# Block transposes of k and x in one VectorE step, exchanged through DRAM, with a new order of work, in an RWKV recurrence fused with a token and channel mixer

## The chip, the cores and the metric

The kernel runs on one core of a Trainium2 chip. The metric is device microseconds of that core, the median of the runs. A core has TensorE (PE in the profile; its weight loads are PEld), VectorE (DVE), ScalarE (ACT), GpSimd (POOL) and SyncE (SP), which here only issues DMAs. Each works through its own list of instructions in order, and waits for the others by semaphores.

## The reference

Four batches, eight heads, 768 steps, 48 channels a head; all is f32.

```python
for t in range(S):
    cur = np.einsum('bhd,bhe->bhde', u[None] * kt, vt)
    y[:, :, t] = np.einsum('bhd,bhde->bhe', rt, state + cur)
    state = wt[:, :, :, None] * state + np.einsum('bhd,bhe->bhde', kt, vt)
...
xt = x.transpose(0, 2, 1)                 # x = y as (4, 768, 384)
h = xt @ U @ V                            # token mix, rank 32
u = x + h.transpose(0, 2, 1)
ch = np.maximum(u @ w_ch1, 0.0) @ w_ch2   # channel mix, 384 -> 1536 -> 384
return (u + ch)
```

## The kernel before

The recurrence is done in 24 chunks of 128 steps (batch b, chunk c, number g = 6b + c), each for all heads: the eight heads lie in pairs j = 0..3, two heads on 128 partitions. For a chunk VectorE makes products of the decays by scans (steps F and Q, lines 390 and 405), r and k are scaled by them (RP, KS), TensorE makes the scores (AM, line 544), VectorE merges them under a mask (CP, line 551), and TensorE makes y from them and v (YA, lines 622 and 632) and from the state of the chunks before (YZ, lines 645 and 649). ScalarE copies y out as x with channels on partitions (XE). The new state needs k with time on partitions: DS (line 561) multiplies it by v, one matmul for each head, with 48 columns of k as the stationary operand; then ZA and ZM add the old state and decay it. The last chunk of a batch makes no state.

Two things are therefore turned from channels-by-time to time-by-channels: k of each chunk for DS (20 chunks), and x of each chunk for the token mix (GA, line 761, then G4, SELM, GS, GSL, once a batch). There are two ways. For early chunks TensorE turns them by transposing matmuls (KT line 522, XT line 735) and ScalarE copies the result out (KN, XN). For the chunks in `TURN_K_DVE` and `TURN_X_DVE`, here 12 to 23, VectorE turns them by blocks of 32 x 32: `turn_blocks` (line 679) and `blocks_of_x` (lines 714 and 716) do a 128 x 128 tile in four steps of four instructions, each from 32 partitions to 32 others, so that each block is turned and put in its place at once.

The 3072 rows of x are cut into seven blocks of 384 or 512 for the channel mix. For each block HP (line 815) makes the token mix, VectorE adds it to x (UADD, line 820), u is split into a high and a low part (UH, UL), UP (line 864) makes 12 products of 9 matmuls, each followed by a ReLU split into high and low (HH on ScalarE line 869 or VectorE line 871, HL line 875), and DN (line 898) makes 3 x 4 products of 9 matmuls, then O (line 916) adds u and OUT sends it. Weights are loaded and split into two parts on the way (LRAW, E, C2, C3, ADD, HI, SUB), and looked at once more later (LCK, CK, CM).

The program is written as some 1400 named steps, each with its engine and the buffers that it takes. The table `ORDER` gives the order in which they are issued, and for each whether it goes to its first engine or to the other one. `plan` replays it: it hands out buffers and refuses an order in which something stands ahead of what it needs. So the order on each engine, SP's DMAs among them, is fixed by hand.

Of the kernel before, what the change touches and what calls it, by code (L numbers as in the profile page):

```python
# [8 lines left out]
F32 = mybir.dt.float32  # L9
# [33 lines left out]
TURN_K_DVE, TURN_X_DVE = [12, 13, 14, 15, 16, 17, 18, 19, 20, 21, 22, 23], [12, 13, 14, 15, 16, 17, 18, 19, 20, 21, 22, 23]  # L43
# [5 lines left out]
def channel_order():  # L49
# [17 lines left out]
    "4S00907X04500D04o15704415804605305400G07Z00A01C00B17v05004q059G0m00X05500H04c04T01A18204704r00e00n00I17u04V0"  # L67
# [3 lines left out]
    "5b11P00k01317w07r08L01f08418A07s08V11K01e01W07t08W11L05l08907p11g00x05m05+08101M08P09e01h05-05o01X08X01N05n0"  # L71
    "8506005p11i05q08615f00y01r01O15c01Y01R01Z08711S01Q08B06102A05g08w01a09E01T08Q05h08S08C01b05d08n08F08T01j08G0"
    "6205e01U01k02B08m08Y16S06309n05x06T08x15r02305y08Z11c15i08o02C01l01s01V15s01t08R02D01u02E05z05u01m05j01y05t0"
    "1n08O01o08p05v05k08c01v05w08u16408a01w06701p08r01x08b01q02402O08D08d01+08y12506501-08E18H06A01z06802H06B0660"
    "2006W09M08v02F02I02608s08z06X08t02706C02102212j02J08+12808e02G18h02P02K08q18i02V02L09206909h08f09009C06a06U0"
# [12 lines left out]
    "G90Az0A+0Do0GA0Dm0Dn0GC0A-0G31GS0G-0I10Dp0Dq0GG0Dr0Ds0Av0B10Dt0Ku0Du0Gv0Gw1Dy0B20Dv0Dw0Dz0D+0GD0E00B30Dx0GB0"
    "E10D-0Gt0Lj0LW0Li0GE0GH0Gc0E20H30LX0B40E30GT1EG0Ga0GV0Gx0LS0E40H41GO0IS0Gu0EH1HM0B50EJ0EI0Gy0GF0E50E60EK0EM0"
    "IT0II0IU0Kw0EL0Ew0Gd0EN0B00Gb1HP0Ge0Lq0G+0EO0EV0Kv0GI0Gf0LT0HQ0Gz1GK0LJ0Ex0H60Gg0EW0Eb0HN0Ec0Aw0ES0EX0Ed0HZ0"  # L90
    "B60IL0E70GJ1EA0E80GL0H50Gh0Gl0LK0Gm0I20Lr0Gi0IV0HA0HU0H70E90H80HR0EB1EP0EC0HS0ED0LL0LU0Ey0ET0Hu0HO0EU0Ls0EQ0"
    "EE1ER0HT0HV0Ha1EY0Gj0L70Hs0Ee0EF0EZ0Ef0HB0Ea0Hc0Gk1Gn0Hb1E+0E-0I30Hv0F00Eg0Hd0Eh0HF0Hx0HG0H90IJ0HC0Hg0HH0Ez1"
    "Ht0L90Ei0Go0He0Ek0Hf0Hh0El0Em0H+1HI0HJ0HD0HK0Hy0Ln0En0F20Eq0F30L80F40I60F10Er0Lt0IK0Gp0Gq0Eo0IW0Hz1I70F50Es0"
    "Hw1FI0Et0I80Hi0I41HL0IA0IX1Eu0Hl0FJ1L40HE1I51Hm0FL0FK0IN0I90IO0F90Ep0FM1Ev0IQ0IP1FR0Hj0IB0IY0Lo0Hk0IC0Gr0FA0"
    "Ej0FN0Hn0FS1IF0FB0ID0Ho0IG0F60IM1Hp0F70F80IZ0FX0FT0FF0Hq0LA0K+0IE1IH0FY0FZ0FO0FG1FH0Hr0Ia0Ib0FP0L50Ih0FC0Ic0"
    "FQ0Id0FD0Lv0Ie0FE0If0Fa0Ig0Fg0Ii0L60Ij0Fb0Ik0Il0LC0Lu0LY0Fc0Im0Fh0In0Ir0Io0Jp0Ip0La0Is0Jq0Iv0Iw0Jt0FU0Ju0FV0"
    "It1FW0Fd0Fe1Iq1M00Fi0Iu0Ff0Fj0Fm0Fn0Fo0Fp0Fq0M20LZ0Fs0Ft0Kx0IR0Ix1Fk0M10Kz0LM0LD0Ky0Iy1Fu0Fv0JC0Kr0Jr0JD1JE0"
    "JR0JS1Lw0Fw0J00Iz0JT0Lz0J11Lp0Kt0J20I+0Jx0JF0I-0JG1J90JH0Jy0LF0JL0JA1J30JB0LN0Lx0LB0Ks0Jv1JM0JU0J40J50L10Js1"
    "JO0JV1Ly0JN0JW0JI0JJ1J60JK0K-0LP0JX0JP1J70J80LE0JQ0Jw0Jz1JY0H-0JZ0Ja0J+1Jd0Je0Jf0Jg0Jj0Jh0Jb0LQ0KQ0Jk0KK0KR1"
# [1125 lines left out]
```

## Time and profile before

| what | us |
|---|---|
| median of 3 runs | 434.61 |
| lowest and highest of them | 434.53, 435.64 |
| span of the profiled execution, first to last instruction | 433.5 |
| PE busy, share | 418.0, 96% |
| PEld busy, share | 363.0, 84% |
| DVE busy, share | 351.0, 81% |
| ACT busy, share | 185.5, 43% |
| POOL busy, share | 134.3, 31% |

The profile gives no separate time of its own execution beside the span; the median of the runs is 1.1 us above it. Its part 2 shows DVE at 9 tenths or more in nearly every slice up to 320 us and at 2 to 7 tenths after that, PE at 9 tenths from 55 us to the end. The granted TensorE clock is 1.00 from 60 us on and 0.94 ahead of that. A busy PE is not a PE at its peak, so what PE could do is read from the starts of its matmuls.

### The profile page before, as it was taken

What the parts mean: (1) busy time and instruction counts of PE and PEld (TensorE: products, weight loads), DVE (VectorE), ACT (ScalarE), POOL (GpSimd) and SP (SyncE); (2) the same over time, 40 slices, a digit from 0 to 9 for tenths busy, and PEclk for the clock granted to TensorE, in tenths of its full rate; (3) what the DMA queues carried; (4) which work ended last, traced back from release to release, by engine and by line L of the source; (5) the groups of instructions that cost most, each with busy time, mean ns of one, the idle gap of its engine ahead of it and who ended that gap; (6) DMA issues with size and microseconds to landing.
All of it is one profiled execution on the core that took longest, in us unless ns stands there. A gap on an engine that the chain in (4) does not pass through costs nothing. (4 is left out here: it accounts for less than half of the span.)

```text
span 433.5 us, 10486 instructions
## 1 busy us (share of the span) xinstructions
PE 418.0 (96%) x4156; PEld 363.0 (84%) x4156; DVE 351.0 (81%) x802; ACT 185.5 (43%) x527; POOL 134.3 (31%) x178
## 2 busy tenths in 40 slices
PE   7987999999999999999999999999989999999994
PEld 5976789999998998787778788888767899999994
DVE  8999999998999999999999999999974237325510
ACT  5999889766443343643044254040332012103400
POOL 5665455635735494322238101041000000000000
PEclk9989899999999999999999999999999999999999
DMA  8989638355826464003226403233002041136001
GB/s 279 327 267 338 204 132 310 110 198 172 272 80 217 123 242 158 23 26 107 98 64 231 119 23 117 81 119 122 8 30 74 1 162 39 36 104 206 2 2 60
DMA packets 23913, 57.29 MB, mean 132 GB/s; under 512 B 2864, under 2 KB 7856, under 8 KB 23856
## 3 DMA queue, kind: packets, MB, share of 16 engines
q1 hardware_dynamic: 23856, 56.54, 39.3%
q8 instruction: 34, 0.56, 0.5%
q14 instruction: 23, 0.19, 0.1%
HBM read 51.81 MB, written 4.72 MB: 130 GB/s over the span
## 5 line engine op out<-in xcount | busy, mean ns | idle before, releaser
L898 PE MATMUL f<-hid,w2h 128*128 128x384 f32 (+1 forms) x504 | 148.5, 364 | 0.0
L864 PE MATMUL f<-u,w1h 128*128 128x384 f32 (+1 forms) x504 | 147.8, 364 | 0.6 <-DVE xT L820 0.3
L864 PEld LDWEIGHTS f<-u,w1h 128*128 128x128 f32 x504 | 92.9, 188 | 12.9 <-issue 1.4
L898 PEld LDWEIGHTS f<-hid,w2h 128*128 128x128 f32 x504 | 92.9, 188 | 10.2 <-issue 0.7
L864 PE MATMUL f<-u,w1l 128*128 128x384 f32 (+1 forms) x252 | 90.8, 360 | 0.0
L898 PE MATMUL f<-hid,w2l 128*128 128x384 f32 (+1 forms) x252 | 90.7, 360 | 0.0
L869 ACT ACTIVATE hid<-f 128x384 fp32r<-128x384 f32 (+1 forms) x60 | 32.2, 538 | 96.9 <-PE f L864 88.9
L875 DVE SCALAR_TENSOR_TENSOR hid<-f,hid 128x384 fp32r<-128x384 f32 (+1 forms) x84 | 50.0, 608 | 11.2 <-ACT hid L869 10.5
L898 PEld LDWEIGHTS f<-hid,w2l 128*128 128x128 f32 x252 | 47.4, 188 | 4.7
L864 PEld LDWEIGHTS f<-u,w1l 128*128 128x128 f32 x252 | 47.4, 188 | 4.0
L679 DVE STREAM_TRANSPOSE kn<-rk 32x128 f32<-32x128 f32 x160 | 48.3, 302 | 2.5
L469 ACT ACTIVATE A<-ident,dv 128x128 f32<-128x128 f32 x140 | 43.8, 391 | 6.0 <-DVE dv L455 4.0
L916 DVE TENSOR_TENSOR xT<-f,xT 128x384 f32<-128x384 f32 (+1 forms) x21 | 12.7, 610 | 38.0 <-PE f L898 37.9
L831 POOL TENSOR_TENSOR u<-xT,u 128x512 fp32r<-128x512 f32 (+1 forms) x10 | 12.3, 1238 | 91.5 <-PE f L864 35.8
L322 POOL TENSOR_TENSOR cva_w<-cva_w,raw_w 128x384 int32<-128x384 int32 x24 | 25.0, 1055 | 41.1 <-DVE cva_w L315 15.7
L405 DVE TENSOR_TENSOR_SCAN Q<-w,starts,qd 128x258 f32<-128x258 f32 x48 | 33.3, 735 | 0.5 <-POOL rk L413 0.2
L551 DVE COPY_PREDICATED A<-maskf,aps 128x1024 f32<-128x1024 uint32 x24 | 31.6, 1315 | 0.4 <-PE aps L544 0.2
L390 DVE TENSOR_TENSOR_SCAN F<-w,qd 128x259 f32<-128x259 f32 x48 | 30.4, 675 | 0.5 <-DMA w<-in_wT 0.4
L716 DVE STREAM_TRANSPOSE xn<-xT 32x192 f32<-32x192 f32 x80 | 29.5, 369 | 1.1
L413 POOL TENSOR_TENSOR rk<-rk,Q 128x512 f32<-128x512 f32 x18 | 21.5, 1193 | 25.4 <-DVE Q L405 25.4
L871 DVE TENSOR_SCALAR hid<-f 128x384 fp32r<-128x384 f32 (+1 forms) x24 | 14.3, 596 | 17.7 <-PE f L864 14.4
L475 POOL TENSOR_SCALAR_AFFINE_SELECT A<-dv 128x128 f32<-128x128 f32 (+1 forms) x39 | 11.7, 333 | 43.1 <-DVE dv L455 20.0
(126 smaller groups left out, 568.2 us busy)
## 6 DMA issues: line engine op xcount, KB each, us to landing
raw_w<-in_w SPq DMA_DIRECT2D x48, 384.0 KB, 3.8
rk<-in_rkT SPq DMA_DIRECT2D x24, 512.0 KB, 5.4
kr<-in_rkN SPq DMA_DIRECT2D x18, 384.0 KB, 4.1
w<-in_wT SPq DMA_DIRECT2D x24, 260.0 KB, 4.0
v<-in_vS SPq DMA_DIRECT2D x24, 224.0 KB, 4.6
out_dram<-xT SPq DMA_DIRECT2D x12, 192.0 KB, 3.5
out_dram<-xT SPq DMA_DIRECT2D x9, 256.0 KB, 4.7
raw_V<-in_V SPq DMA_DIRECT2D x8, 96.0 KB, 3.8
```

The lines of the kernel that those rows point to most:

```text
L322: lambda: nc.gpsimd.tensor_tensor(out=d["to"].bitcast(I32), in0=d["a"].bitcast(I32), in1=d["e"], op=ALU.add),
L390: nc.vector.tensor_tensor_scan(out=back(F), data0=back(st["w"]), data1=back(qd, OVER * h), initial=1.0, op0=ALU.mult, op1=ALU.add)
L405: nc.vector.tensor_tensor_scan(out=st["Q"][:, a:e], data0=st["w"][:, a:e], data1=qd[:, a - OVER * h : e - OVER * h], initial=starts[:, h : ...
L413: ENG[eng].tensor_tensor(out=rk[:, 0], in0=rk[:, 0], in1=Qv, op=ALU.mult)
L469: nc.scalar.activation(to, one, AF.Copy, scale=dv[:, NP * i + j : NP * i + j + 1])
L551: nc.vector.copy_predicated(to, mask2, new)
L679: nc.vector.transpose(to[32 * j : 32 * j + 32, :, 32 * i : 32 * i + 32], src[32 * i : 32 * i + 32, :, 32 * j : 32 * j + 32])
L716: nc.vector.transpose(to[q, :, :, r], src[r, :, :, q])
L864: nc.tensor.matmul(ps, wt[:, f, ct, :], u[ct][:, z], start=(m == 0), stop=(m == 8))
L869: nc.scalar.activation(h[:, 0], d["ps", f], AF.Relu)
L875: nc.vector.scalar_tensor_tensor(out=h[:, 1], in0=d["ps", f], scalar=0.0, in1=h[:, 0].bitcast(F32), op0=ALU.max, op1=ALU.subtract)
L898: nc.tensor.matmul(d["o", ct], wt[:, 4 * ct + part, f - 3 * part, :], hid[f][:, z], start=(part == 0 and m == 0), stop=(part == 3 and m == 8),
```

## The change

k of chunks 9, 10, 12 to 16 and 18 to 22, and x of chunks 9 to 23, are now turned in three steps. One VectorE instruction turns each 32 x 32 block where it lies, on all 128 partitions (KB for k; XB1 or XB2 for x of one or two chunks). One DMA writes that to a tile in DRAM (KW, XW), and four DMAs read it back with the blocks exchanged (KL, XL). The turned tiles are laid out by quarters of the channels, so DS takes 32 channels at a time: 16 matmuls with 32 stationary columns in place of 8 with 48. GA reads x in the new layout and GS puts its columns back in order. Chunks 9 to 11 thereby leave TensorE's transposes. On PE the table differs from the fourth UP product of block 0 on. `CHOICES` lets a step have more than one other engine, which no step here uses, and the step that loads the flag (PF) must now stand ahead of the last O.

```diff
-TURN_K_DVE, TURN_X_DVE = [12, 13, 14, 15, 16, 17, 18, 19, 20, 21, 22, 23], [12, 13, 14, 15, 16, 17, 18, 19, 20, 21, 22, 23]
+TURN_K_DVE, TURN_X_DVE = [9, 10, 11, 12, 13, 14, 15, 16, 17, 18, 19, 20, 21, 22, 23], [9, 10, 11, 12, 13, 14, 15, 16, 17, 18, 19, 20, 21, 22, 23]
...
-    "0t07y11107m05N08U05O01201I07+00i07n05P08N07k07l00j05QC0w07-15R01J05U05S07q07Y15V05W05Y05Z01d05a05T18807o05X1"
+    "0t07y11107m05N08U05O01201I07+00i07n05P08N07k07l00j05QI0w07-15R01J05U05S07q07Y15V05W05Y05Z01d05a05T18807o05X1"
...
-        def turn_k_blocks(i):
-            if i == 0:
-                st["kn"] = place("kn", [P, NP, P], f"kn_{g}", buf["kn"])
-            turn_blocks(st["kn"], st["rk"][:, 1], i)
+        def turn_k_blocks():
+            d = st["kt"] = place("big", [P, 4, NP, 32], f"kt_{g}", btk)
+            nc.vector.transpose(d.rearrange("p b j c -> p j b c"), st["rk"][:, 1].rearrange("p j (b c) -> p j b c", c=32))
+
+        def send_k():
+            st["kd"] = dram.tile([4, 32, 4, NP * 32], F32, name=f"kd_{g}")
+            nc.sync.dma_start(st["kd"].rearrange("q a b x -> (q a) (b x)"), st["kt"].rearrange("p b j c -> p (b j c)"))
+
+        def fetch_k():
+            st["kn"] = place("kn", [P, 4, NP, 32], f"kn_{g}", buf["kn"])
+            for i in range(4):
+                nc.sync.dma_start(
+                    st["kn"][32 * i : 32 * i + 32].rearrange("a q j c -> a q (j c)"),
+                    st["kd"][:, :, i].rearrange("q a x -> a q x"),
+                )
...
-                for i in range(2):
-                    r = slice(64 * i, 64 * i + D)
+                for q in range(4):
+                    i = q // 2
+                    r = slice(32 * q, 32 * q + 32)
                     to = dS[r, j, i * D : i * D + D]
...
-                    nc.tensor.matmul(to, kn[:, j, r], v[:, j, r], start=not z_pe, stop=True)
+                    nc.tensor.matmul(to, kn[:, q, j, :], v[:, j, 64 * i : 64 * i + D], start=not z_pe, stop=True)
...
-                kn = ks
-                for i in range(4):
-                    kn = step(
-                        "KD " + nm, "DVE", lambda i=i: turn_k_blocks(i), [kn], take=[buf["kn"]] if i == 0 else [],
-                        use=[buf["rk"], buf["kn"]],
-                    )
+                btk = Buf("big")
+                kn = step("KB " + nm, "DVE", turn_k_blocks, [ks], take=[btk], use=[buf["rk"]])
+                kn = step("KW " + nm, "SP", send_k, [kn], use=[btk])
+                kn = step("KL " + nm, "SP", fetch_k, [kn], take=[buf["kn"]])
...
+            def blocks_of_x():
+                t = d["xt"] = place("big", [P, n, 4, NCT, 32], f"xt_{b}_{c}", btx)
+                for m in range(n):
+                    src = blocks[blk][:, :, (cc + 1 - n + m) * P : (cc + 2 - n + m) * P]
+                    nc.vector.transpose(
+                        t[:, m].rearrange("p b a c -> p a b c"), src.rearrange("p a (b c) -> p a b c", c=32)
+                    )
...
+            xb = step(f"XB{n} {b}.{c}", "DVE", blocks_of_x, after, take=[btx], use=[bx])
+            xw = step(f"XW{n} {b}.{c}", "SP", send_x, [xb], use=[btx])
+            xl = step(
+                f"XL{n} {b}.{c}", "SP", fetch_x, [xw] + ([even["first"]] if even and n == 1 else []),
+                take=[bxn] if n == 2 else take, use=[bxn],
+            )
```

Three places show how the order moves. The first is PE at the end of batch 2. `f_2_1` and `f_2_2` are two of the three output tiles of block 2 in DN, `ga` is GA (`xn_2` holds x of chunks 16 and 17), `aps` AM of the next chunk, `gb` SELM; before:

```order
L898 MATMUL f_2_1_3198<-hid_11_3097,w2h 128x512
L761 MATMUL ga_3266<-xn_0_2648,U_sb 32x384 x2
L761 MATMUL ga_3266<-xn_1_3055,U_sb 32x384 x2
L761 MATMUL ga_3266<-xn_2_3227,U_sb 32x192 x4
L544 MATMUL aps<-rk_3114 64x128 x4
...
L772 MATMUL gb_3317<-g_2_3299,sel 96x384
```

and now:

```order
L922 MATMUL f_2_1_3382<-hid_11_2822,w2h 128x512
L637 MATMUL y_3435<-A_3245,v_3006 32x128 x8
L647 MATMUL y_3435<-A_3245,v_3006 32x128 x8
L785 MATMUL ga_3453<-xn_0_3196,U_sb 32x384 x2
L785 MATMUL ga_3453<-xn_1_3255,U_sb 32x384 x2
L785 MATMUL ga_3453<-xn_2_3399,U_sb 32x192 x4
L560 MATMUL aps<-rk_3378 64x128 x4
...
L796 MATMUL gb_3482<-g_2_3462,sel 96x384
```

YA 18 now stands between the last DN product and GA, and AM between GA and SELM is that of chunk 19. Ahead of the first row lie, now, YZ 17 and AM 18 and then the four DN products of `f_2_1`; before, YZ 17, one DN product and these four.

The second is PE at the end of batch 3, GA (`ga`), SELM (`gb`) and HP (`hp`); before:

```order
L649 MATMUL y_4367<-rk_3899,Z_4276 32x128 x4
L761 MATMUL ga_4399<-xn_0_3931,U_sb 32x384 x2
L761 MATMUL ga_4399<-xn_1_3975,U_sb 32x384 x2
L864 MATMUL f_4_2_4404<-u_0_3756,w1h 128x512
...
L898 MATMUL f_4_0_4447<-hid_2_4421,w2h 128x512
L761 MATMUL ga_4399<-xn_2_4416,U_sb 32x192 x4
L772 MATMUL gb_4466<-g_3_4462,sel 96x384
L898 MATMUL f_4_0_4447<-hid_3_4360,w2h 128x512
...
L815 MATMUL hp_0_4485<-Vst,gs_4468 128x384
L815 MATMUL hp_1_4487<-Vst,gs_4468 128x384
L815 MATMUL hp_0_4490<-Vst,gs_4468 128x384
```

and now:

```order
L922 MATMUL f_4_1_4584<-hid_11_4074,w2h 128x512
L785 MATMUL ga_4637<-xn_0_4621,U_sb 32x384 x2
L785 MATMUL ga_4637<-xn_1_4628,U_sb 32x384 x2
L785 MATMUL ga_4637<-xn_2_4642,U_sb 32x192 x4
L922 MATMUL f_4_2_4654<-hid_0_4265,w2h 128x512
...
L796 MATMUL gb_4666<-g_3_4664,sel 96x384
L922 MATMUL f_4_2_4654<-hid_3_4152,w2h 128x512
...
L839 MATMUL hp_0_4680<-Vst,gs_4677 128x384
L839 MATMUL hp_1_4686<-Vst,gs_4677 128x384
L922 MATMUL f_4_2_4654<-hid_6_4341,w2h 128x512
```

GA now has one UP and eight DN products of block 4 between it and the last y, a DN product between it and SELM, and DN products among HP, where five HP stood in a row.

The third is SP around the exchange of x of chunks 16 and 17 (`xd_5`, `xn_2`) and of k of chunk 18 (`kd`, `kn`), now; `raw` are the weights that are looked at once more:

```order
L362 DMA w_3376<-in_wT 128x520
L366 DMA rk_3378<-in_rkT 128x1024
L724 DMA xd_5_3397<-xt_5_3357 128x2x384
L734 DMA xn_2_3399<-xd_5_3397 32x8x96 x4
L287 DMA raw_V_3404<-in_V 32x768
L370 DMA kr_3490<-in_rkN 128x768
L287 DMA raw_w_7_3515<-in_w 128x768
L533 DMA kd_3536<-kt_3406 128x512
L287 DMA raw_w_1_3541<-in_w 128x768
L538 DMA kn_3544<-kd_3536 32x4x128 x4
```

Before, SP's list held only loads and outputs; now a write waits there for VectorE and a read for that write, with the next loads behind both.

## Rows read from the trace of the kernel before

**Rows 1.** Windows: stretch, PE, PEld, DVE, ACT, POOL busy (instructions), clock, DMA, GB/s

```profile
160.00:340.00 180.00, 176.36 (x1626) 140.31 (x1617) 162.50 (x386) 60.59 (x168) 41.70 (x59) 1.00 0.28 90
340.00:428.00 88.00, 87.94 (x489) 84.81 (x488) 34.95 (x79) 14.76 (x43) 1.02 (x1) 1.00 0.22 73
```

**Rows 2.** Timeline, the end: start us, length us, engine, line, instruction

```profile
427.97 0.56 DVE L916 TENSOR_TENSOR xT<-f,xT 128x384 f32<-128x384 f32 x1 [5.61 <-PE f L898]
428.56 0.33 SPq L919 DMA_DIRECT2D out_dram<-xT  x1
```

**Rows 3.** Waits of PEld from 60 to 430 us: total us, times, longest

```profile
PEld ga L761 <- DVE xn L716: 2.1, 2, 1.1
...
PEld hp L815 <- DVE xT L820: 1.5, 3, 0.8
...
PEld f L864 <- DVE hid L875: 1.3, 4, 0.7
PEld f L864 <- DVE xT L820: 1.0, 2, 0.7
PEld gb L772 <- ACT g L767: 1.0, 1, 1.0
```

**Rows 4.** Timeline of PE at the end of batch 2

```profile
214.39 0.39 PE L898 MATMUL f<-hid,w2l 128*128 128x512 f32 x1
214.62 0.85 PE L898 MATMUL f<-hid,w2h 128*128 128x512 f32 x3
215.40 0.85 PE L761 MATMUL ga<-xn,U_sb 128*32 128x384 f32 x8
216.59 0.53 PE L761 MATMUL ga<-xn,U_sb 128*32 128x192 f32 x8 [0.34 <-DVE xn L716]
217.05 0.90 PE L544 MATMUL aps<-rk 48*64 48x128 f32 x32
```

**Rows 5.** Groups by form, DVE: count, busy us, mean ns, idle before

```profile
L679 DVE STREAM_TRANSPOSE kn<-rk 32x128 f32<-32x128 f32 x160 | 48.3, 302 | 2.5
L716 DVE STREAM_TRANSPOSE xn<-xT 32x192 f32<-32x192 f32 x80 | 29.5, 369 | 1.1
L714 DVE STREAM_TRANSPOSE xn<-xT 32x96 f32<-32x96 f32 x32 | 8.6, 269 | 0.4
...
L820 DVE TENSOR_TENSOR xT<-hp,xT 128x384 f32<-128x384 f32 x12 | 6.3, 550 | 1.3 <-PE hp L815 1.2
...
L781 DVE TENSOR_TENSOR gs<-gb,gs 32x384 fp32r<-32x384 f32 x4 | 2.2, 555 | 0.5 <-ACT gs L776 0.4
```

**Rows 6.** Timeline of PE: KT 7, DS 6, AM 7, XT of chunk 6, UP of block 0

```profile
57.31 0.60 PE L522 MATMUL trk<-ident,rk 128*128 128x128 f32 x4
57.84 0.56 PE L561 MATMUL dS<-v,kn 128*48 128x48 f32 x16
58.33 0.90 PE L544 MATMUL aps<-rk 48*64 48x128 f32 x32
59.16 0.55 PE L735 MATMUL trx<-ident,xT 128*128 128x128 f32 x3
59.46 0.42 PE L864 MATMUL f<-u,w1h 128*128 128x384 f32 x1
59.72 0.34 PE L864 MATMUL f<-u,w1l 128*128 128x384 f32 x1
59.90 0.34 PE L864 MATMUL f<-u,w1h 128*128 128x384 f32 x1
```

**Rows 7.** Timeline of PE: YA 18

```profile
239.74 0.65 PE L622 MATMUL y<-A,v 128*32 128x128 f32 x16
240.21 0.62 PE L632 MATMUL y<-A,v 128*32 128x128 f32 x16
```

**Rows 8.** DMA issues by line: count, KB each, median us to landing

```profile
out_dram<-xT SPq DMA_DIRECT2D x12, 192.0 KB, 3.5
out_dram<-xT SPq DMA_DIRECT2D x9, 256.0 KB, 4.7
raw_V<-in_V SPq DMA_DIRECT2D x8, 96.0 KB, 3.8
```

**Rows 9.** Timeline of ACT: XE 17 behind YZ 17

```profile
205.03 0.49 ACT L666 ACTIVATE xT<-y 128x384 f32<-128x384 f32 x1 [5.16 <-PE y L649]
```

More of the change, by code (lines that the diff above doesn't have):

```diff
@@ L71 @@
[L71 to L75, printed above, removed]
@@ L242, in step @@
     def step(name, eng, fn, after=(), take=(), use=(), alt=None):
-        s = Step(name, eng, fn, after, list(take), list(use), alt)
+        s = Step(name, eng, fn, after, list(take), list(use), alt.split() if alt else None)
         steps.append(s)
@@ L353, in chunk @@
         nm = str(g)
-        by_pe = g < 6
+        by_pe = g in DIAG_PE
         def load_w():
@@ L674, in rwkv_moe_kernel @@
     block_of = lambda g: max(n for n in range(NB) if STARTS[n] <= g * P)
-    def turn_blocks(to, src, i):
-        for j in range(4):
-            nc.vector.transpose(
-                to[32 * j : 32 * j + 32, :, 32 * i : 32 * i + 32], src[32 * i : 32 * i + 32, :, 32 * j : 32 * j + 32]
-            )
     def turn(b, c, blk, cc, after, bx):
@@ L692, in hold @@
             if "both" not in e:
-                e["both"] = place("xn", [P, 2, NCT, P], f"xn_{b}_{c // 2}", bxn)
+                e["both"] = place("xn", [P, 2, 4, NCT, 32], f"xn_{b}_{c // 2}", bxn)
             xns[b, c]["xn"] = e["both"][:, c % 2]
@@ L707, in blocks_of_x @@
                     hold(c - 1)
-                to = both[:, c % 2 + 1 - n : c % 2 + 1]
-                src = blocks[blk][:, :, (cc + 1 - n) * P : (cc + 1) * P].rearrange("p a (n t) -> p n a t", t=P)
-                for j in range(4):
-                    q = slice(32 * j, 32 * j + 32)
-                    r = slice(32 * i, 32 * i + 32)
-                    if n == 1:
-                        nc.vector.transpose(to[q, 0, :, r], src[r, 0, :, q])
-                    else:
-                        nc.vector.transpose(to[q, :, :, r], src[r, :, :, q])
-            last = after + ([even["first"]] if even and n == 1 else [])
-            for i in range(4):
-                last = [step(
-                    f"XD{n} {b}.{c}", "DVE", lambda i=i: blocks_of_x(i), last,
-                    take=([bxn] if n == 2 else take) if i == 0 else [], use=[bx, bxn],
-                )]
-                d.setdefault("first", last[0])
+                to = both[:, c % 2 + 1 - n : c % 2 + 1].rearrange("p m q a c -> p (m q) (a c)")
+                for i in range(4):
+                    nc.sync.dma_start(to[32 * i : 32 * i + 32], d["xd"][:, :, :, i].rearrange("m q a x -> a (m q) x"))
+            xb = step(f"XB{n} {b}.{c}", "DVE", blocks_of_x, after, take=[btx], use=[bx])
[3 more added lines that the diff above has]
+                take=[bxn] if n == 2 else take, use=[bxn],
+            )
+            d["first"] = xl
+            last = [xl]
             d["steps"] = last
@@ L1135, in rwkv_moe_kernel @@
     outs[NB - 1, NCT - 1][1].after.append(pd)
-    step("PF", "SP", fetch, [pd])
+    outs[NB - 1, NCT - 1][-1].after.append(step("PF", "SP", fetch, [pd]))
     with tc.manual_schedule():
```

98 lines of the change are left out of this document (59 added, 39 removed).

## The prediction, made before the changed kernel was run

> **What bounds the kernel now.** Read the busy shares last and the starts of PE's matmuls first. The page has PE at 96% and DVE at 81%, and part 2 shows DVE full up to 320 us and half idle after that. One could think that DVE sets the pace. But windows of PE, then its timeline, then its waits say otherwise. From 340 us on only the channel mix is left, and PE is busy for 87.9 of 88 us [rows 1], a matmul of 384 columns starting 0.18 us after the one before [rows 6]. In the stretch from 160 to 340 us, where DVE is busy for 162.5 of 180 us, PE is busy for 176.4 [rows 1], and its 512-column matmuls start every 0.23 us there [rows 4], as fast as they ever do. So PE is full nearly all the way, and DVE only just keeps up with it. What DVE costs is what PE waits for it, and that is little: from 60 us on the weight loads waited 2.1 us for x to be turned (ahead of GA), 1.5 and 1.0 us for the chain from HP over UADD to the next HP or UP, 1.0 us for ScalarE's copy between GA and SELM, and 1.3 us for HL [rows 3]. These are 6.9 us of 434. The first four, 5.6 us, come mostly at a batch's end, where PE has nothing else in line. The first 59 us hold more idle time, but there every step on PE stands as before.
>
> The end is fixed: the last O starts at 427.97 us, the output is issued at 428.56 [rows 2], and the rest to 433.5 is the output landing and the close. Whatever PE saves moves this tail as it is.
>
> **The change, part by part.**
>
> *VectorE.* It loses all of its small transposes, 160, 80 and 32 of them, 86.4 us in all [rows 5]. What one large one takes no row shows. Over 96, 128 and 192 elements a partition the small ones take 269, 302 and 369 ns [rows 5], which is 1.04 ns an element over a fixed part. That gives 0.70 us for 512 elements, 0.97 for 768 and 0.57 for 384, if 128 partitions cost what 32 do; 32 x 384 and 128 x 384 of two other operations take 555 and 550 ns [rows 5], so I take that. Then 12 k (8.4 us), 6 pairs of x (5.8) and 3 single x (1.7) cost 16 us. At four times that, quarter after quarter, it would be 64 us. The order also hands DVE about 15 us more (eight HH, six ZM, three RP, and some more), so it falls from 351 to about 295 us. Worth on the path: only the waits above, not 56 us.
>
> *PE's own work.* Two turns of k and three of x leave PE (chunk 11 ends a batch and needs no k). One of k takes 57.84 - 57.31 = 0.53 us, one of x 59.46 - 59.16 = 0.30 [rows 6]: 2 x 0.53 + 3 x 0.30 = **-2.0 us**. The new order also goes from the channel mix to small products and back 23 times in place of 28 (counted on PE from the third UP product on). The first matmul after such a change takes 0.26 us in place of 0.18 [rows 6], so 5 x 0.08 = **-0.4 us**.
>
> *DS.* 16 matmuls become 32 in the profile's count (an f32 product runs as two). Today 16, with 48 stationary and 48 moving columns, take 0.49 us [rows 6]. YA has 32 stationary columns, as the new DS will; there 16 matmuls with 128 moving columns take 0.47 us [rows 7], that is 16 x 128 / 0.47 = 4.4 columns a ns, four side by side. At this rate 32 x 48 columns take 0.35 us and a start-up beside it: no more than now. The other end is twice today's 0.49. I take **0**, since YA has the same form.
>
> [...] The trace has 16 of DS in 0.49 us and 32 of AM in 0.83 us, 26 to 31 ns each, so no row here goes below that on average. [...]
>
> *Waits that go.* At batch 3 eight DN products and one UP now stand between the last y and GA, a DN product (2.07 us) between GA and SELM, where the copy takes 0.5, and more among HP; at batch 2 AM stands there. At each of the four kinds PE has other work in line, so I take away all of their 5.6 us: **-5.6**. The least is 0 (the waits come back elsewhere), the most 6.9.
>
> *Waits that come.* A turn now needs two transfers in a row. Nearest rows: writing 192 and 256 KB lands after 3.5 and 4.7 us, reading 96 KB after 3.8 [rows 8]. For a pair of x (384 KB) that is 4.7 us at least, 7.1 by the step between the two rows, and then 3.8. The tight place is the end of batch 2. From the end of YZ 17 the path is XE 0.49 [rows 9], XB 0.97, the write, the read, and 0.3 for three hand-overs: 10.3 to 12.7 us. PE has in line AM (0.83), four DN products (4 x 2.07), YA (0.94) and the first half of GA (0.8): 10.9. So GA waits 0 to 1.8 us: **+0.9**. At the end of batches 1 and 3 there are nine products of the channel mix or more in line, 14 to 19 us. k has room too: KB waits for no state and stands far ahead of its DS.
>
> SP runs its list in order, so a load behind XW or KL starts when VectorE, or the write, is done. Behind the exchange in the third place that the change shows stand the look at V, kr of chunk 20 and k of chunk 18; none is needed by the next products on PE. What is late next is no engine's sum but single steps that stand tight behind each other: CP for YA, HL for DN. HL's 1.3 us stay; I add the same again for new ones: **+1.3**, between 0 and four times that.
>
> *Sum.* -2.0 - 0.4 - 5.6 + 0.9 + 1.3 = -5.8 us. The profiled execution spans 433.5 us, so 427.7; the median of the runs lies 1.1 us above that span, so **428.8 us**, 1.3% faster.
>
> **The rivals.**
>
> *The waits come back.* The exchanges, SP's blocked list, or large transposes at four times the price (DVE then again at some 345 us) cost what the four kinds of waits gave. Then only the 2.4 us of PE's own work remain: 432.2, and with the new waits of the sum 434.4. For it: 21 round trips of some 8.5 us or more where there were none. Against it: all but one have far more than that in line. Chance 0.14.
>
> *DS runs two at a time.* If matmuls with 32 stationary columns find no fourfold room when they move only 48, DS takes 0.98 us. 15 of the 20 DS lie behind 57 us, where PE is full: 15 x 0.49 = 7.4 us, so 436.2, **slower**. It eats the whole gain from 0.39 us a DS on (5.8 / 15). For it: no row has short matmuls with 32 stationary columns. Against it: YA's rate. Chance 0.09.
>
> *PE has room.* PEld is busy for 140.3 of 180 us in the stretch from 160 to 340 us and for 84.8 of 88 at the end [rows 1]. If that difference were idle time, 180 x (0.96 - 0.78) = 33 us were to be had, and the kernel would come to about 401 (434.6 - 33). Against it: nine loads go with each 512-column product as with each 384-column one, and the matmuls of 512 start 0.23 us apart without a pause [rows 4]. Chance 0.02. [...]
>
> **How the numbers follow.** The forecast has 0.75. Its best case has no new waits and all 6.9 us gone: -9.3, 425.3; its worst has 1.8 and 5.2 us of new waits: -1.0, 433.6. The range, 425.3 to 434.4, takes in these and most of the first rival; outside are the second, the third and a rest. A measurement of this kernel can tell about 0.3%, 1.3 us, from no change. Faster by more than that, below 433.3: 0.74 of the forecast, the third rival and a third of the first, 0.80. Within 0.3%: the rest of the first rival and a tail of the forecast, 0.11. Slower: 0.09.
>
> **What would show it.** Right: the last O at about 422.5 us; the large transposes near 0.70 and 0.97 us and DVE near 295 us busy with 30% idle; DS from its first matmul to the next product about 0.5 us; no wait of GA or HP over 1 us but at batch 2; PE's 512-column matmuls still 0.23 us apart. Wrong: DS at 0.8 to 1.0 us (second rival); waits of PE for DMAs of xn or kn, or for loads that stood behind them on SP (first rival); transposes near 2.8 us; or less than 0.3% saved though the waits are gone, which would mean that PE's products themselves became slower.

## The result, and the profile after

The changed kernel takes 432.8 us (median of 8 runs, 428.4 to 438.5) against 435.25 us before (8 runs, 434.5 to 436.7): ratio 0.9913, 95% interval 0.9888 to 0.9938. Run again, beside other runs of before, it took 434.6 us (10 runs, 430.2 to 437.1): 0.994, interval 0.9907 to 0.9972. So it is 0.6 to 0.9% faster, where 1.3% was forecast, and its times spread over 10 us where those of the kernel before spread over 3 (87 runs in all, 434.25 to 437.6). The ratios leave out executions more than 1.5% above the fastest, here five of 18 between 436.8 and 438.5; they belong to the spread that has to be explained.

The first profiled execution (428.41 us) is the fastest of all. The stretches of [rows 1] in it:

```profile
160.00:340.00 180.00, 179.91 (x1836) 145.70 (x1824) 116.22 (x206) 53.66 (x152) 39.23 (x60) 1.00 0.53 162
340.00:428.00 88.00, 80.97 (x460) 79.31 (x458) 31.63 (x68) 10.89 (x28) 3.01 (x3) 0.98 0.07 26
```

VectorE has gone from 162.5 to 116.2 us between 160 and 340 us, PE from 176.4 to 179.9 of 180. The DMA share has nearly doubled, 0.28 to 0.53. The end, against [rows 2]:

```profile
421.07 0.56 DVE L940 TENSOR_TENSOR xT<-f,xT 128x384 f32<-128x384 f32 x1 [5.75 <-PE f L922]
421.66 0.33 SPq L943 DMA_DIRECT2D out_dram<-xT  x1
```

The last O comes 6.9 us earlier. The waits of the weight loads from 60 to 430 us, against [rows 3]:

```profile
PEld aps L560 <- issue: 2.9, 10, 0.6
PEld y L637 <- DVE A L567: 1.8, 1, 1.8
PEld ga L785 <- issue: 1.4, 6, 0.4
PEld f L888 <- DVE hid L899: 1.3, 5, 0.4
```

No wait of GA, HP or SELM for another engine is left; HL's 1.3 us stands as before, and there is one new wait, 1.8 us of YA for CP of chunk 9. At the end of batch 2 GA follows YA without a pause, where [rows 4] had 0.34 us, and the 512-column products ahead of it start every 0.23 us as there:

```profile
214.10 0.39 PE L922 MATMUL f<-hid,w2l 128*128 128x512 f32 x1
214.33 0.85 PE L922 MATMUL f<-hid,w2h 128*128 128x512 f32 x3
215.11 0.65 PE L637 MATMUL y<-A,v 128*32 128x128 f32 x16
215.57 0.62 PE L647 MATMUL y<-A,v 128*32 128x128 f32 x16
216.01 1.15 PE L785 MATMUL ga<-xn,U_sb 128*32 128x384 f32 x16
217.09 0.90 PE L560 MATMUL aps<-rk 48*64 48x128 f32 x32
```

The large transposes (groups by form, columns as in [rows 5]), and KT, DS and AM (PE's timeline, as in [rows 6]):

```profile
L529 DVE STREAM_TRANSPOSE kt<-rk 128x512 f32<-128x512 f32 x12 | 8.4, 699 | 0.3 <-POOL rk L423 0.2
L718 DVE STREAM_TRANSPOSE xt<-xT 128x384 f32<-128x384 f32 x15 | 8.0, 557 | 2.7 <-ACT xT L681 2.7
```
```profile
57.07 0.60 PE L525 MATMUL trk<-ident,rk 128*128 128x128 f32 x4
57.60 0.55 PE L578 MATMUL dS<-v,kn 128*32 128x48 f32 x32
58.08 0.90 PE L560 MATMUL aps<-rk 48*64 48x128 f32 x32
```

So this execution did what was forecast. The question is why the others take 2 to 10 us more.

### The profile page after: what moved, and what is told of

Its sections match the earlier page's. It is cut to its first block, busy times and chain, and to the rows that moved or that the text cites. A ratio compares the mean times of both kernels' runs of the same rounds, so it can differ in the third digit from the quotient of the medians.

```text
span 426.6 us, 11108 instructions
## 1 busy us (share of the span) xinstructions
PE 411.9 (97%) x4523; PEld 359.9 (84%) x4523; DVE 298.0 (70%) x584; ACT 168.6 (40%) x480; POOL 127.9 (30%) x173
## 2 busy tenths in 40 slices
DMA packets 42875, 69.51 MB, mean 163 GB/s; under 512 B 12225, under 2 KB 25281, under 8 KB 42817
## 4 chain that ended last, share of the span: by engine, by line
PE 80%; ACT 8%; DVE 5%; DMA 4%; issue 1%; POOL 1%; SPq 0%; DVEq 0%; POOLq 0%
PE f L888 34%; PE f L922 31%; PE aps L560 3%; ACT A L472 3%; DMA raw_w<-in_w 2%; PE y L637 2%; PE y L647 2%; PE y L660 1%; PE dS L578 1%; DMA kr<-in_rkN 1%; PE hp L839 1%; ACT Z L617 1%; ACT raw_w L312 1%; PE ga L785 1%; PE gb L796 1%
## 5 line engine op out<-in xcount | busy, mean ns | idle before, releaser
L922 PE MATMUL f<-hid,w2h 128*128 128x384 f32 (+1 forms) x504 | 145.7, 363 | 0.0
L893 ACT ACTIVATE hid<-f 128x384 fp32r<-128x384 f32 (+1 forms) x52 | 27.4, 535 | 116.8 <-PE f L888 105.5
L472 ACT ACTIVATE A<-ident,dv 128x128 f32<-128x128 f32 x132 | 41.1, 390 | 2.6 <-PE f L888 1.8
L325 POOL TENSOR_TENSOR cva_w<-cva_w,raw_w 128x384 int32<-128x384 int32 x24 | 26.0, 1095 | 35.8 <-DVE cva_w L318 10.8
L895 DVE TENSOR_SCALAR hid<-f 128x384 fp32r<-128x384 f32 (+1 forms) x32 | 19.4, 610 | 9.6 <-PE f L888 7.8
L560 PEld LDWEIGHTS aps<-rk 48*64 48x64 f32 x768 | 20.8, 147 | 6.1 <-issue 3.8
L416 POOL TENSOR_TENSOR rk<-rk,Q 128x512 f32<-128x512 f32 x15 | 18.1, 1210 | 25.4 <-DMA rk<-in_rkT 17.6
L560 PE MATMUL aps<-rk 48*64 48x128 f32 (+1 forms) x768 | 24.3, 270 | 1.3 <-POOL rk L416 0.9
L432 ACT ACTIVATE junk<-w,b_max 128x512 uint8<-128x512 uint32 x24 | 17.2, 717 | 15.5 <-DMA w<-in_wT 15.4
```

The source lines that it names most:

```text
L325: lambda: nc.gpsimd.tensor_tensor(out=d["to"].bitcast(I32), in0=d["a"].bitcast(I32), in1=d["e"], op=ALU.add),
L416: ENG[eng].tensor_tensor(out=rk[:, 0], in0=rk[:, 0], in1=Qv, op=ALU.mult)
L472: nc.scalar.activation(to, one, AF.Copy, scale=dv[:, NP * i + j : NP * i + j + 1])
L560: nc.tensor.matmul(aps[HP * a : HP * a + HP, i, jj, s0:P], rk[r, 1, jj, k0 : k0 + HP], rk[r, 0, jj, s0:P], start=True, stop=True,)
L893: nc.scalar.activation(h[:, 0], d["ps", f], AF.Relu)
L895: nc.vector.tensor_scalar(out=h[:, 0], in0=d["ps", f], scalar1=0.0, scalar2=None, op0=ALU.max)
```

## The experiments

All were timed against the kernel before on the same chip.

**The changed kernel again** (no edit).

> The changed kernel once more, unaltered, to see another profile and more times. Its first eight runs spread over 10 us (428.4 to 438.5) where the kernel before spreads over 2. Theory A (the waits that come are in the stretch from 60 to 120 us, where VectorE is full and the weights' loads land late): a slower execution shows its added stalls of PE there, and the last stretches (160 to 340, 340 to the end) are as long as in the first profile, within 1 us. Theory B (the exchanges of k and x through DRAM land late): the added stalls stand ahead of DS and GA, between 110 and 330 us. Times by both: 428 to 435.

Both theories missed the place. The profiled execution took 437.1 us, and most of the loss stands before 56 us, ahead of all that the change moves. PE's waits there, and its timeline around the first and in front of the second:

```profile
PE y L647 <- issue: 2.1, 1, 2.1
PE dS L578 <- issue: 1.3, 1, 1.3
```
```profile
32.83 0.92 PE L647 MATMUL y<-A,v 128*32 128x128 f32 x10
35.83 0.31 PE L647 MATMUL y<-A,v 128*32 128x128 f32 x3 [2.08 <-issue]
...
45.13 0.30 PE L577 MATMUL dS<-Z,ident 128*32 128x48 f32 x7 [0.96 <-ACT Z L617]
```

"issue" is a wait for nothing that the profile shows, in the middle of a YA and of a DS. Counted over PE's rows in the trace (matmuls, weight loads and the few rows of its sequencer), the two stalls come after 961 and 1473 of them, and a shorter one in the next experiment's profile (0.6 us, inside an AM) after 1217: exactly 256 apart. What comes in such pieces is PE's own instructions:

```profile
PE 417.8 (96%) x4523; PEld 363.5 (83%) x4523; DVE 298.4 (69%) x584; ACT 168.9 (39%) x480; POOL 128.9 (30%) x173
...
q1 hardware_dynamic: 42816, 68.74, 49.8%
q8 instruction: 37, 0.61, 0.6%
```

The queue q8 carries 37 packets with 0.61 MB, 16 KB each, for 9046 matmuls and weight loads; before it was 34 for 8312, and DS in 32 columns is what has more. I call 256 such rows, with the packet that brings them, a block, and the counts its edges; that they belong together is read from these numbers. In the first profile one packet of q8 lands 0.9 to 3.6 us behind each of the eleven edges from 193 (961 less 3 x 256) to 2753. Here the packets ahead of the two stalls landed at 34.45 and 45.97 us, and PE went on 1.4 and 1.3 us after each. In the first profile the former of the two had landed at 29.36, when PE had done 773 rows. Counted from the edge before it (row 705), that block took 7.4 us to land here and 1.6 us there, and PE had used up the 256 rows between the two edges in 6.7 us. Behind the stalls PE's clock falls (windows, columns as in [rows 1]; first this execution, then the first profile):

```profile
44.00:47.00 3.00, 1.09 (x66) 0.78 (x58) 2.82 (x5) 2.28 (x9) 2.85 (x4) 1.00 0.57 209
47.00:54.00 7.00, 6.70 (x100) 5.29 (x100) 3.71 (x8) 3.28 (x10) 0.00 (x0) 0.51 0.28 77
```
```profile
44.00:47.00 3.00, 3.00 (x88) 2.81 (x84) 3.00 (x6) 2.93 (x9) 3.00 (x4) 0.69 0.08 12
47.00:54.00 7.00, 6.67 (x133) 4.63 (x122) 7.00 (x18) 6.24 (x19) 1.42 (x3) 1.00 0.95 310
```

PE stands for most of 44 to 47 us, 0.96 us of it for ScalarE's Z and the rest for its instructions, and then runs at a granted clock of 0.51 for 7 us, with VectorE half idle behind it (3.7 of 7). The first UP product starts at 65.2 us in place of 59.2: 3.4 us of stalls, the rest mostly the clock by these windows. The exchange's traffic has no part in this: its first transfer is issued at 95 us here, and at 88 us or later in every profile.

**The reads not waiting for the writes.**

```diff
-                    st["kd"][:, :, i].rearrange("q a x -> a q x"),
+                    rkT[b, c].rearrange("(q a) z j t -> a q (z j t)", q=4)[:, :, P * i : P * i + P],
```

and the same for x, from `rkN`.

> The reads of the exchange take the same sizes and pieces from inputs, not from what was just written, and so don't wait for the write (k and x are then not the turned ones, and what is computed from them is not the reference's); writes and the amount of traffic stay. Theory B (exchanges land late): faster than the changed kernel by 2 us or more, and its spread falls from some 6 us to 2 or less. Theory A (the stretch from 60 to 120 us): the same time and the same spread within 1 us, since the tight steps there wait for weights and scans, not for turned k or x.

434.65 us (430.9 to 437.0), ratio 0.9985 (0.9961 to 1.0009). The latency of the exchange does not make the loss: GA and DS don't wait less for it (GA 0.6 us here; none in the first profile of the changed kernel, 0.4 us in the second), since they hardly waited.

**The order alone.** In place of KB and XB, KW and XW, KL and XL, four steps of four small transposes stand where KL and XL stood:

```diff
-                kn = step("KB " + nm, "DVE", turn_k_blocks, [ks], take=[btk], use=[buf["rk"]])
...
+                for i in range(4):
+                    kn = step(
+                        "KD " + nm, "DVE", lambda i=i: turn_k_blocks(i), [kn], take=[buf["kn"]] if i == 0 else [],
+                        use=[buf["rk"], buf["kn"]],
+                    )
```

> The new order with the old small transposes: chunks 9 on are turned by sixteen small transposes for each k and for each x or pair of x, at the place where the read of the exchange stood; no exchange. VectorE gets some 90 us more than in the changed kernel, with about 50 of them between 160 and 340 us (116 to about 165 us busy of 180). Theory 1 (VectorE costs only what PE waits for, and the order takes these waits away): 430 to 436 us, at most 3 us above the changed kernel. Rival 2 (VectorE's relief is what pays, the order only makes room for it): PE waits for x at the ends of the batches again, 4 us a time and more, so 437 to 450.

503.35 us (501.0 to 505.1), ratio 1.157: beyond both. PE's waits from 57 us on (total, times, longest):

```profile
PE ga L771 <- DVE xT L926: 10.4, 1, 10.4
PE f L874 <- DVE hid L885: 8.1, 3, 3.5
PE dS L572 <- DVE kn L532: 5.8, 3, 3.6
PE ga L771 <- DVE xn L719: 4.7, 2, 4.5
```

VectorE is busy for 388.6 us, 90 more than in the changed kernel, and PE's clock averages 0.91 between 160 and 340 us. The new order only works with the cheap turns. It was not planned for the dear ones, so this says nothing of the best order that they could have. Its profile also has two stalls at a block's edge, one of 1.0 us behind 1217 rows and one of 0.5 us behind 1473, in a kernel that exchanges nothing.

**The exchange alone**, in the order of before, chunks 12 on: KB and KW at the place of the first KD, KL at that of the last, and so for x.

```diff
-TURN_K_DVE, TURN_X_DVE = [9, 10, 11, 12, 13, ...], [9, 10, 11, 12, 13, ...]
+TURN_K_DVE, TURN_X_DVE = [12, 13, ...], [12, 13, ...]
```

> The exchange alone, for chunks 12 on, in the order of before: one large transpose and the write where the first small transpose stood, the reads where the last one stood. VectorE falls by about 60 us. Theory 1 (only the waits count): GA now waits for a whole exchange of x, some 8 to 10 us, at the ends of batches 2 and 3, and smaller waits come at DS, so it is slower than before: 440 to 460. Rival 2 (VectorE's relief is what pays): 428 to 434 in spite of these waits.

436.9 us (434.3 to 442.3), 1.0042 (1.0015 to 1.007). VectorE falls to 277.7 us and nothing is gained, but little is lost: PE waited 2.4 us for `kn` and 0.3 for `xn`, not 8 to 10 at GA, so nearly all of an exchange was covered by other work. Of these two runs neither part gains alone, and the spread is there (8 us) without the new order.

**DS in its old form for chunks 0 to 8.** Where PE turns k, `kn` is kept as before and DS goes in pieces of 48 again:

```diff
+                if g not in TURN_K_DVE:
+                    for i in range(2):
+                        r = slice(64 * i, 64 * i + D)
+                        to = dS[r, j, i * D : i * D + D]
...
+                        nc.tensor.matmul(to, kn[:, j, r], v[:, j, r], start=not z_pe, stop=True)
+                    continue
```

> The changed kernel, but DS of the chunks that PE turns (0 to 8) has its old form again: stationary columns in pieces of 48, 16 matmuls (32 where Z is added by PE) in place of 32 (64). Theory S (PE runs out of instructions in the first 57 us: its small products there need twice as many for DS, and in the slower profile PE waited 2.1 and 1.3 us for nothing but its own instructions, ahead of YA and inside a DS at 43 to 47 us, and the clock fell behind that): the spread shrinks from some 7 us to 3 or less, the fastest run stays near 428 to 430 and the median falls to 428 to 431. Theory C (the clock falls in the first 57 us at random, whatever DS looks like): median 432 to 435 and a spread of 6 us or more, as now.

432.07 us (6 runs, 429.15 to 433.2), 0.9915 (0.9892 to 0.9938). The spread shrinks to 4 us in these six runs; the median lies where theory C had it, and the interval is nearly that of the changed kernel's first set, so a gain of the median is not shown. Its profile has one block's stall, 1.1 us long after 4289 rows (16 x 256 more than 193; 961 is 3 x 256 more), at 163 us, inside an UP product, and the wait for CP 9 that the changed kernel has too:

```profile
PE y L643 <- DVE A L565: 1.3, 1, 1.3
PE f L894 <- issue: 1.1, 1, 1.1
```

**The kernel before with DS in 32 columns.**

```diff
-                for i in range(2):
-                    r = slice(64 * i, 64 * i + D)
+                for q in range(4):
+                    i = q // 2
+                    r = slice(32 * q, 32 * q + 32)
```

> The kernel before with one thing changed: DS in pieces of 32 columns, 32 matmuls (64 where Z is added by PE) in place of 16 (32), in the same order and with nothing exchanged. Theory S (PE's supply of instructions in the first 57 us): its runs spread as far as those of the changed kernel, 5 us or more where before has 3, and the median is 1 to 3 us above before, 436 to 438. Theory C (the new order has less slack behind the first 57 us, so that what varies there shows at the end): 434 to 436.5 and a spread of 3 us, like before.

435.45 us (434.7 to 440.1, eleven of twelve below 436.9), 1.0008 (0.9987 to 1.003): no change. In the old order, with its lighter DMA traffic (a share of 0.28 from 160 to 340 us in the kernel before, 0.53 in the changed), the doubled instructions of DS cost nothing on the median. That speaks against theory S alone; time and spread, but for one run, are those of theory C. The exchange alone, in much the same order and with the same DS, spread over 8 us: in the old order the spread came with the exchange, not with DS.

**Fewer packets, then no exchange.** First the reads take whole rows, as written:

```diff
-                    st["kn"][32 * i : 32 * i + 32].rearrange("a q j c -> a q (j c)"),
-                    st["kd"][:, :, i].rearrange("q a x -> a q x"),
+                    st["kn"][32 * i : 32 * i + 32].rearrange("a q j c -> a (q j c)"),
+                    st["kd"][i].rearrange("a b x -> a (b x)"),
```

> The changed kernel, but the exchange is read back row by row as it was written (k and x stay turned within their blocks of 32 only, so what is computed from them is not the reference's): the same bytes, issues and waits, in a quarter of the packets for the reads, of 1.5 to 2 KB in place of 384 to 512 bytes. Theory T (the exchange's small packets keep the DMA engines busy, and PE's instruction blocks of 16 KB, which come through the same engines, land late: PE stood still at its 961st, 1217th, 1473rd and 4289th instruction, 256 or a multiple of it apart): the DMA share between 160 and 340 us falls from 0.53 to about 0.45, the median falls by 1 to 3 us to 430 to 432, and the spread from 7 us to 4 or less. Theory S (only the supply in the first 57 us matters): as the changed kernel, 431 to 435, spread 6 us or more.

432.1 us (430.5 to 434.6), 0.993 (0.9904 to 0.9955); the packets fall from 42,875 to 32,506, but the DMA share from 160 to 340 us only from 0.53 to 0.51. The median fits theory T, but 432 is also in the range of S, and the traffic hardly fell, so this run decides little. Then POOL fills the tiles, and one row of each write is left:

```diff
-            for i in range(4):
-                nc.sync.dma_start(
...
+            nc.gpsimd.memset(st["kn"], 0.5)
```

> The changed kernel without the exchange: of each write one row of 2 KB is left, the reads are gone, and POOL fills the tiles with a constant at the place of the reads (the new state and the tokens' mix then come from that constant). The DMA share between 160 and 340 us falls from 0.53 to about 0.2, and POOL gets some 12 us. Theory T (the exchange's traffic delays instructions): 427 to 430, spread 3 us or less. Theory S (the supply in the first 57 us, where no exchange runs): 430 to 435, spread 6 us or more, with stalls of PE at a block's edge before 57 us. Theory C (the new order has no slack left behind a start that varies for reasons of its own): like S, but without such stalls.

430.3 us (429.1 to 434.0), 0.9896 (0.9862 to 0.993), DMA share 0.35. That is 2.5 and 4.3 us under the two medians of the changed kernel, with an interval that overlaps those of both sets: the exchange's traffic may cost something, but these runs don't show it. The spread, 5 us, lies between the theories. The profile's first UP starts at 61.7 us, 2.5 us later than in the first profile, and ahead of it PE has no wait on "issue": a late start without a block's stall, as theory C had it.

**CP 9 ahead**, with the old DS early: one step moved in the order.

```diff
-k09U02l09V06i0BA06k06l09L02m02n02o02p0940980
+k09409U02l09V06i0BA06k06l09L02m02n02o02p0980
```

> The kernel with the old DS for chunks 0 to 8, and CP of chunk 9 four steps further ahead on VectorE, before the transpose of k of chunk 10, C2 and C3 of w2 piece 10 and RP of chunk 10 (2.7 us of work). In the profiles of both kernels PE waits 1.3 to 1.7 us for this CP ahead of YA 9, the longest wait of PE for another engine's work behind 57 us. If that is on the path: 1 to 1.7 us below the one with the old DS alone, that is a median of 430 to 431. Rival: VectorE is full in this stretch, and RP 10, which is now later, or HL of the first UP products of block 1 makes PE wait as long: 432, no change.

429.16 us (4 runs, 428.3 to 429.8), 0.9858 (0.9837 to 0.9878): the wait of YA was on the path, and it is gone from the profile. The median fell by 2.9 us, more than the 1.3 us of the wait, so the rest has another cause or is chance. The profile, the slowest of the four, has two waits of PE between 140 and 170 us:

```profile
PE ga L791 <- DMA xn<-xd: 1.8, 1, 1.8
PE f L894 <- issue: 1.6, 1, 1.6
```

The second again stands after 4289 rows. Its block landed at 163.0 us, and PE went on at 164.4. The DMA engines were nearly full around it (windows):

```profile
154.00:162.00 8.00, 8.00 (x175) 7.03 (x174) 6.93 (x14) 1.72 (x5) 4.26 (x7) 1.00 0.87 265
162.00:168.00 6.00, 4.38 (x20) 3.28 (x19) 4.97 (x8) 3.05 (x10) 3.27 (x6) 1.00 0.84 283
```

**Four second looks at the weights later** (LCK, CK and CM of pieces 18, 25, 20 and 9, moved in the order from 148 to 156 us to behind LCK 13, at 341 us).

> The kernel with the old DS early and CP 9 ahead, and the second looks at four pieces of w1 and w2 (384 KB each, loaded at 148 to 156 us) moved with their reductions to 341 us and later, where the DMA engines are idle. In the profile without this, the DMA engines are busy for 0.9 and more from 154 to 166 us, a block of 16 KB of PE's instructions arrives at 163.0 us, and PE stands still for 2.0 us until 164.4 at its 4289th instruction, inside a product of the channel mix. Theory T (data in front of an instruction block): that stall goes or falls under 0.5 us, and the median falls by 1 to 2 us, to 427 to 428.2. Rival (the block comes late whatever the traffic, since it is asked for late): the stall at the 4289th instruction stays at 1.4 to 2.0 us and the time at 429.

428.88 us (6 runs, 426.8 to 431.5), 0.986 (0.9833 to 0.9886). The profile is the fastest of its runs. In it the block landed at 158.7 us, 4.4 us earlier, while PE was 70 rows short of the edge, and PE has no stall: from 60 to 430 us it waits nowhere by the profile's count. The windows:

```profile
154.00:162.00 8.00, 8.00 (x173) 6.84 (x172) 7.90 (x17) 2.77 (x8) 4.27 (x8) 1.00 0.81 248
162.00:168.00 6.00, 6.00 (x27) 4.72 (x26) 3.72 (x7) 2.31 (x7) 2.73 (x3) 1.00 0.45 152
```

Of the 4.4 us PE itself gave 1.7: without GA's wait it reached the edge before (row 4033) at 156.6 us in place of 158.3. From there the block took 2.0 us to land in place of 4.7. So the stall went as theory T says, in this profile and the next, though not by the traffic alone; the median did not fall by the 1 to 2 us, so it may not stand in every execution of the kernel before it. GA's wait is gone too, though the first load moved was issued at 148.6 us, when PE was already waiting (148.2 to 149.9 us). It varies where these loads stand as before: 0 in the first profile and with the old DS alone, 0.4 us in the changed kernel run again, 1.4 with fewer packets.

**The load of r and k of chunk 15 behind the read of x** (LRK 15 moved behind XL2 1.5, on top).

> As the kernel with the looks late, and the load of r and k of chunk 15 (512 KB), which stood on SP between the write and the read of the last x of batch 1, issued behind that read. In the profile with CP 9 ahead, GA of batch 1 waited 1.4 us for that read. If the load's traffic delays the exchange: the wait shrinks to under 0.7 us and the time falls by another 0.5 to 1 us. Rival (the load comes 5 us later and KS 15 on POOL, or a step behind it, is late): no change or up to 2 us slower.

428.25 us (5 runs, 426.8 to 429.8), 0.9843 (0.9822 to 0.9864). The wait that this step was to shorten (1.8 us in the profile, not 1.4) was already gone in the profile before. Against the last two the intervals overlap; the step itself is not shown to gain. It is the best version found, 1.6% faster than before, with nothing left out:

```profile
419.14 0.56 DVE L946 TENSOR_TENSOR xT<-f,xT 128x384 f32<-128x384 f32 x1 [5.75 <-PE f L928]
419.73 0.33 SPq L949 DMA_DIRECT2D out_dram<-xT  x1
```

**The early DS in 32 columns put back** into this version (its edit above undone).

> The best kernel so far (old DS for chunks 0 to 8, CP 9 ahead, four looks late, r and k of chunk 15 behind x; 426.8 to 429.8) with one thing put back: DS in 32 columns for chunks 0 to 8 too. Theory S (in the first 57 us PE uses its instructions up faster with this DS than they come): the spread goes back to 5 us or more and the median rises by 1 us or more, to 429.3 to 432; a slow execution shows PE standing still with no releaser at its 961st, 1217th or 1473rd instruction. Rival (the early DS never mattered, and the kernel with the old DS alone was faster by chance): median 427.5 to 429, and a spread of 3 us.

430.21 us (6 runs, 429.0 to 432.2), 0.9883 (0.9858 to 0.9908), against 0.9843 (0.9822 to 0.9864): 2 us slower, as expected, with intervals that just overlap and a spread of 3 us, less than expected. Its profile (431.5 us, where the one before is 426.8) has no stall at a block's edge before 56 us, and its first UP comes only 0.4 us later. The other 4.1 us stand behind that, most of them in waits for VectorE that the one before does not have:

```profile
PE f L888 <- DVE xT L940: 1.4, 1, 1.4
PE f L922 <- DVE w2l L342: 0.8, 2, 0.5
```

So this execution did not lose its time where theory S says, and what cost the 2 us of the median is not shown.

The profiles' landmarks in us, side by side:

| kernel | first UP | from there to the last O | last O to the end |
|---|---|---|---|
| before | 59.5 | 368.5 | 5.6 |
| before, DS 32 | 59.9 | 368.0 | 5.6 |
| changed, first profile | 59.2 | 361.9 | 5.5 |
| changed, again | 65.2 | 364.0 | 6.2 |
| no waiting for writes | 58.5 | 363.1 | 7.5 |
| fewer packets | 60.5 | 364.3 | 5.5 |
| no exchange | 61.7 | 361.3 | 6.1 |
| old DS early | 58.7 | 362.7 | 6.0 |
| and CP 9 ahead | 58.7 | 363.7 | 5.7 |
| and looks late | 58.6 | 360.5 | 5.6 |
| and r, k behind x | 58.9 | 360.3 | 5.6 |
| last, DS 32 early | 59.3 | 364.4 | 5.8 |

With the old DS early four profiles reach the first UP within 0.3 us of each other; with DS in 32 columns and the new order six spread from 58.5 to 65.2. What the three late ones share (65.2, 61.7 and 60.5) is not a stall at a block's edge, which only the first of them has, but the clock: between 36 and 56 us it stands at 0.5 for some 7 us or more in each, and for half as long or not at all in the others. And the clock does not need such a stall to fall. With fewer packets PE waited for ScalarE's Z until 42 us and the clock fell; with CP 9 ahead it waited as long there and the clock stayed up (the wait and windows of the one, then of the other):

```profile
PE dS L577 <- ACT Z L617: 3.0, 1, 3.0
42.00:45.00 3.00, 2.80 (x79) 2.36 (x83) 3.00 (x6) 2.36 (x8) 3.00 (x4) 0.50 0.46 164
45.00:48.00 3.00, 3.00 (x68) 2.73 (x66) 2.45 (x5) 1.76 (x5) 1.89 (x3) 0.50 0.32 89
```
```profile
PE dS L575 <- ACT Z L623: 2.9, 1, 2.9
42.00:45.00 3.00, 3.00 (x105) 2.71 (x103) 3.00 (x6) 2.58 (x8) 3.00 (x4) 1.00 0.36 135
45.00:48.00 3.00, 2.32 (x73) 1.88 (x67) 3.00 (x6) 3.00 (x10) 1.53 (x3) 1.00 0.53 175
```

The middle stretch can be read the same way, by laying the starts of PE's products side by side with those of the profile with the looks late. What a profile takes longer stands at a few places, each with a wait in PE's list: CP for YA 9 (1.3 to 1.5 us wherever CP 9 is not ahead), the read of x for GA at batch 1 (0 to 1.8), the stall after 4289 rows (1.1 and 1.6), and waits of up to 1.4 us for VectorE and ScalarE. For the changed kernel run again these are mainly YA 9, GA, one DN and one YA. Why these waits differ from one execution to the next is not shown.

## Why the prediction was right or wrong

**The sum was right for the best execution.** Between the first UP and the last O the change saved 368.5 - 361.9 = 6.6 us, and the sum said 5.8 (which puts the last O at 422.2 us, not at the 422.5 that I wrote). The difference is about the wait that I gave GA at batch 2, 0.9 us: it was 0. An x pair's write landed after a median of 2.8 us and a read after 2.8, where I took 4.7 to 7.1 and 3.8 from other transfers. The waits that go (5.6 us) went; of new ones YA's 1.8 us is the only large one, against 1.3 forecast. The large transposes took 0.70 us for k and 0.56 for one x, twice for a pair (1.1 against 0.97), and VectorE 298 us against 295. DS took 0.55 us in the row, as [rows 6] had 0.56: 0 was right for its time, and the second rival fell. From DS's first start to AM's first are 0.48 us for 32 matmuls, 15 ns each, where the prediction's rows had 26 to 31. Three figures of the prediction were my estimates, shown by no row. That YA's matmuls run four side by side was read from its rate alone, 4.4 columns a ns against 0.97 for KT (4 x 128 columns in 0.53 us, [rows 6]). The 0.8 us from which a DS was to count for the second rival is below the 0.98 us of two at a time. And of the 0.3 us for three hand-overs, the one from XB to XW took 0.03 us in the first profile (chunks 16 and 17). The third rival had nothing for it: the 512-column products still start every 0.23 us.

**The median was wrong by 4 to 6 us**, inside the range for the first set of runs and just past its edge for the second. That the range holds the first set is luck: its upper part was there for the first rival. The step that failed is the sentence that the first 59 us hold "more idle time, but there every step on PE stands as before", together with the price of DS. The DS of that stretch are doubled too. I priced them as time on PE and found none, and the exchange's transfers by who waits for the data, and found 0.9 us. Neither has a term for PE's instructions, which come in a DMA queue of their own (q8, 37 packets of 16 KB where before had 34, in a kernel that moves 12 MB more), or for how much a start varies. In their place the runs show a first UP between 58.5 and 65.2 us, and a middle of 361.3 to 364.4 us where the first profile had 361.9.

How much of this is the instructions is shown in part. Shown are the stalls at the blocks' edges (after 961, 1217, 1473 and 4289 rows), 0.5 to 2.1 us each, in five profiles. Of the seven profiles of the new order with this DS, three have such stalls in the first 59 us. Shown is also that the clock was low behind the stalls of the changed kernel run again (0.51 for 7 us), but elsewhere it was low without them (0.50 with fewer packets). Not shown are the two prices from timed runs, 2 us for the early DS in the improved order (none in the old one) and 2.5 to 4 us for the exchange's traffic: in both the intervals overlap. That traffic delays a block is supported by the stall that went when four loads were moved (2.0 us from the edge before to the landing, in place of 4.7). Theory C, a start that varies for reasons of its own and an order with less slack behind it, was never ruled out: it foretold the kernel before with DS in 32 columns, and the late starts without a block's stall, though not that the spread shrank with the old DS. So the cause of the median stays open. Open are also the 5.5 to 7.5 us behind the last O, which no kernel tried to change.

**The first rival** has the right time for many runs (432.2 to 434.4) and the wrong mechanism: in the two profiles of the changed kernel PE waited 0.4 us in all for the exchange, and reads that wait for no write gained nothing. In variants GA waited up to 1.8 us, at batch 1, where I had seen 14 to 19 us of other work in line, and not at batch 2, which I had called the tight place. My expectations of the order alone and of the exchange alone missed as well. I had said VectorE's relief was worth "only the waits above"; with this order and without the relief, PE waits for VectorE at GA (10.4 us once), DS (5.8) and UP (8.1).

## What to carry to other kernels

A stall with no releaser in the middle of a product can be the engine's own instructions: here such stalls stood a multiple of 256 rows apart, and each ended 1.3 to 1.5 us after a packet of 16 KB had landed in an instruction queue. Count the rows up to a stall and look for a multiple of one number between such stalls, and when a change doubles the instructions of dense small products, or fills the DMA engines, give the supply a term of its own (the stalls here took 0.5 to 2.1 us each). Loads that nobody needs soon need not stand where the DMA engines are full (0.84 to 0.87 busy here); moving four took a stall out of the profile, with no gain of the median shown. Before naming one cause for a spread, lay several profiles side by side, product by product: here the late starts shared the clock (0.5 for some 7 us or more) and not the stall. And judge a change by many executions: the first profile was the best of 18, and the sum that fitted it told nothing of the others.

## What was not expected of the hardware

PE resumed 1.3 to 1.5 us after its block of instructions had landed, in seven stalls of five profiles, and in no profile sooner than that. The 32 matmuls of a DS with 32 stationary columns start 15 ns apart on average (0.48 us from DS's first start to AM's, first profile). There a round trip through DRAM lands after 4.2 + 3.1 us for k and 2.8 + 2.8 for a pair of x (medians):

```profile
kd<-kt SPq DMA_DIRECT2D x12, 256.0 KB, 4.2
kn<-kd SPq DMA_DIRECT2D x48, 64.0 KB, 3.1
...
xd<-xt SPq DMA_DIRECT2D x6, 384.0 KB, 2.8
xn<-xd SPq DMA_DIRECT2D x24, 96.0 KB, 2.8
```
